# Top-k attention and an ELU layer on one core: weights decoded in two passes, and the first eight steps in written order

## The chip, the cores and the metric

The kernel runs on one core of a Trainium2 chip. The metric is the device time of one execution in microseconds (us), the median of several runs. Engines are called as in the profile: PE (TensorE, matrix products), PEld (its weight loads), DVE (VectorE), ACT (ScalarE), POOL (GpSimd) and SP (SyncE, which issues nearly all DMAs here). Each engine works through its own queue in order and waits at an instruction until what it needs from other engines is there.

## The reference

Attention over 8 batches, 8 heads, 576 tokens and 64 elements per head, in which each query keeps only the 32 largest scores of its row; then a layer with an ELU between two products.

```python
scores = scale * np.matmul(q, k.transpose(0, 1, 3, 2))        # (8, 8, 576, 576)
kth = np.partition(scores, -32, axis=-1)[..., -32:-31]
scores = np.where(scores >= kth, scores, -1e9)
attn = np.exp(scores - max); attn = attn / (sum + 1e-9)        # max and sum along the row
x = np.matmul(attn, v)           # then (B,H,S,D) -> (4608, 512)
h = x @ w_in                     # (4608, 512) @ (512, 2048)
g = np.where(h > 0.0, h, np.exp(np.minimum(h, 0.0)) - 1.0)
out = (g @ w_out).astype(np.float32)   # (4608, 2048) @ (2048, 512)
```

q, k and v are float32. `w_in` and `w_out` come as float64 (a float32 array times a float64 scalar); the kernel sees each as pairs of 32-bit words and makes float32 of them on the chip. This is the decoding that the change is about.

## The kernel before

**Steps.** A step is one tile of 128 queries for a pair of heads, so two rows of 128 x 576 scores, called row 0 and row 1 here. There are 144 steps. The first 16 take batch 0's four tiles one after the other, four head pairs each, so that the first tile's rows of x are complete after four steps and the second product's work can begin. `tight` is 8: the first eight steps have a code of their own.

**What a step goes through.** `scores` (L322) has PE multiply q by k, and ACT copy the result with the scale into an SBUF tile `sc`. The selection on DVE finds the 32nd largest score: four times the eight largest (MAX8), and between them three times the replacement of those eight by -1e30 (MATCH_REPLACE8, into `wk`). `mask` (L389) has ACT do Prelu and Exp per row, with the sum in `den`; in the first steps ACT also computes the gap between the largest and the 32nd score (L404), later POOL does (L406). `normalise` (L412) is POOL's: the reciprocal of the sum, and two multiplications of 128 x 576. `turn` (L429) transposes the row pair on PE, in nine blocks, and ACT copies them to `et`. `attend` (L454) multiplies by v on PE, and `finish` has ACT copy the result to `xT`. When a block of queries is complete, `ffn_pieces` (L521) adds its 16 pieces `hidden` (product with `w_in`, three ACT operations for each four, a gate that DVE adds up at L517, or POOL) and four `project` per 128 queries (product with `w_out`) to the list `ffn`.

**Feeding.** `feed` (L661) is called four times in a step. It takes pieces from `ffn` at a pace that spreads the work up to the time when the next block is ready (`ready`, in steps), and takes none whose weights are not decoded yet (`decoded`). It also closes gates that were opened `keep` calls before.

**Decoding.** The 32 pieces of weights (16 of each matrix, 512 KB of words, 128 x 512 results) pass through `decode_piece(i)` (L211), which loads piece i+3 and does one stage each of several pieces: `convert_first` of piece i (POOL clamps the upper words, L176), `convert_second` of piece i-1 (ACT: L182 makes a float of the lower words, L183 takes the absolute value of the upper ones into the place of the lower, L185 writes the sign into the top byte of each result), `convert_third` of piece i-3 (DVE shifts, L189), `convert_last` of piece i-4 (POOL adds, L193). Eight buffers hold raw pieces. `hook` (L199) runs the next such call: four times a step in steps 0 to 6 (after the second and third replacement of each row), not in step 7, three times a step from step 8 on. From piece 28 on, the last two stages lie one call later. There are 37 calls, so the decoding ends in step 10.

**Order.** Around the first eight steps there is no written order: the framework's scheduler places the instructions of PE, ACT, DVE and POOL, and may bring an instruction forward past others. In these steps one row is selected after the other in the program (`select_row`), both rows are masked in the same step, the transposes of step n are in the middle of step n+1, and scores are computed three steps ahead. From step 8 on (L729), the four engines run in the order that the program is written in (`manual_schedule`): both rows in turns (`select`), row 0 masked after the first pass of the next step and row 1 after the second, normalised at that step's end, and transposed a step later still. SP's order is the scheduler's throughout.

Of the kernel before, what the change touches and what calls it, by code (L numbers as in the profile page):

```python
# [10 lines left out]
FP32 = mybir.dt.float32  # L11
U32 = mybir.dt.uint32
I32 = mybir.dt.int32
FP8 = mybir.dt.float8e4
PSUM = bass.MemoryType.PSUM

TOP_K = 32
# [64 lines left out]
def kernel(  # L82
# [94 lines left out]

    def convert_second(i):
        lo, hi = parts(raw[i])
        ef = hi.bitcast(FP32)  # L180
        w = weight(i)[1]
        nc.scalar.activation(w, lo, AF.Copy, scale=2.0**-35, bias=2.0**17)  # L182
        nc.scalar.activation(lo.bitcast(FP32), ef, AF.Abs, scale=2.0**-112)  # L183
        signs = w.bitcast(FP8).rearrange("p (n w) -> p n w", w=4)[:, :, 3]
        nc.scalar.activation(signs, ef, AF.Copy, scale=2.0**-30, saturate=False)  # L185

    def convert_third(i):
        lo = parts(raw[i])[0]
# [5 lines left out]

    decode = []
    decoded = [0]
    scheduled = 4 * (2 * NHP - 1)

    def hook():  # L199

# [10 lines left out]
    def decode_piece(i):  # L211
        if i + 3 < 2 * NF:
            load_weight(i + 3)
        apart = 1 if i >= scheduled else 0
        stages = [(0, convert_first), (1, convert_second)]
        if i != scheduled:
            stages += [(3 + apart, convert_third), (4 + apart, convert_last)]
        for ago, stage in stages:
            if 0 <= i - ago < 2 * NF:
                stage(i - ago)  # L220
        decoded[0] = max(0, i - 3 - apart)

    loaded, kqT, vT = {}, {}, {}

# [85 lines left out]
    def start_qk(b, hp):  # L310
        turning.append(transpose_qk(b, hp))
# [29 lines left out]
                wide[i][:, :, 0:HS], AF.Copy, scale=scale,  # L341
            )

    def select_row(u, i, decoding):
        if i == 0:
            u.first = small.tile([P, 2, 8], FP32, tag="m1", name="m1")
            u.last = small.tile([P, 2, 8], FP32, tag="m4", name="m4")
        sc = u.sc[:, i, :]
        m = u.first[:, i, :]
        nc.vector.max(m, sc)  # L350
        wk = wkpool.tile([P, S], FP32, tag=f"wk{i}", name="wk")
        cur = sc
        for r in range(TOP_K // 8 - 1):
            nc.vector.match_replace(wk[:], m, cur, TAKEN)
            cur = wk[:]
            if r < TOP_K // 8 - 2:
                m = small.tile([P, 8], FP32, tag=f"m{i}", name="m")[:]
            else:
                m = u.last[:, i, :]
            nc.vector.max(m, cur)  # L360
            if r > 0 and decoding:
                hook()
            if r != 1:
                yield

    def select(u):

        u.first = small.tile([P, 2, 8], FP32, tag="m1", name="m1")
        u.last = small.tile([P, 2, 8], FP32, tag="m4", name="m4")
        cur = [u.sc[:, i, :] for i in range(2)]  # L370
        found = [u.first[:, i, :] for i in range(2)]
        for i in range(2):
            nc.vector.max(found[i], cur[i])  # L373
        yield
        wk = [wkpool.tile([P, S], FP32, tag=f"wk{i}", name="wk")[:] for i in range(2)]
        for r in range(TOP_K // 8 - 1):
            for i in range(2):
                nc.vector.match_replace(wk[i], found[i], cur[i], TAKEN)  # L378
            cur = wk
            for i in range(2):  # L380
                if r < TOP_K // 8 - 2:
                    found[i] = small.tile([P, 8], FP32, tag=f"m{i}", name="m")[:]
                else:
                    found[i] = u.last[:, i, :]
                nc.vector.max(found[i], cur[i])  # L385
            hook()
            yield
# [214 lines left out]
    for b in range(B):  # L602
        if b % 2 == 0:
            rest = 2 * J
            division = [(0,), (1,), (2,), (3,), (rest,), (4, 5), (6, 7)]
            if b > 0:
                division = [(0, 1), (2, 3), (rest, 4, 5), (6, 7)]
            slots = {}
            for part in division:
                blk = Block(len(blocks), len(part))  # L610
                blocks.append(blk)
                slots.update((x, (blk, s)) for s, x in enumerate(part))
        first[b] = len(steps)
        tiles = []
        for qt in range(J + 1):
            r0 = b * S + (JP if qt == J else qt if b == 0 else qt * P)
            if qt == J:
                (blk, slot), c0, n = slots[rest], (b % 2) * R, R
                rows = slice(r0, r0 + R)
            else:  # L620
                (blk, slot), c0, n = slots[(b % 2) * J + qt], 0, P
                rows = slice(r0, r0 + J * (P - 1) + 1, J) if b == 0 else slice(r0, r0 + P)
            c0 += slot * P
            t = Tile(b, qt, rows, blk, slice(c0, c0 + n))
            blk.left += NHP
            blk.tiles[slot].append(t)
            tiles.append(t)
        order = [(0, 1), (2, 3), (J,)] if b % 2 == 0 else [(J,), (0, 1), (2, 3)]
        if b == 0:
            order[:2] = [(0,), (1,), (2,), (3,)]  # L630
        for qts in order:
            for hp in range(NHP // 2 if qts == (J,) else NHP):
                group = Group([tiles[qt] for qt in qts], hp)
                steps += [Step(tiles[qt], hp, group, i) for i, qt in enumerate(qts)]
            for qt in qts:
                n = len(steps)
                tiles[qt].block.ready = n + 1.0 if n <= tight else n + 2.5
    NS = len(steps)
    total = 0.0
    for blk in sorted(blocks, key=lambda x: x.ready):  # L640
# [20 lines left out]
    def feed(n, share):  # L661

        place[0] += 1
        close_gates(2 if n < tight - 1 or n > tight + 1 else 6)
        fed["at"] = max(fed["at"], n)
        ahead = [(w - fed["sum"]) / (x - fed["at"]) for x, w in due if x > fed["at"]]
        if ahead:
            fed["over"] += max(0.0, share * min(ahead))
        fed["at"] += share
        while ffn and decoded[0] >= ffn[0][1] and 0.5 * ffn[0][0] <= fed["over"]:  # L670
            cost, _, piece = ffn.pop(0)
            fed["over"] -= cost
            fed["sum"] += cost
            piece()

    E = mybir.EngineType
    engines = {E.PE, E.Activation, E.DVE, E.Pool}
    load_qk(0, 0, nc.scalar)
    load_weight(0)
    load_qk(0, 1)  # L680
    load_weight(1)
    load_v(0, 0)
    load_weight(2)
    with tc.manual_schedule(engines=engines):
        for hp in range(2):
            start_qk(0, hp)
            turn_qk(True)
            scores(steps[hp])
    load_qk(0, 2)
    load_qk(0, 3)  # L690
    for hp in range(1, NHP):
        load_v(0, hp)
    decode += [lambda i=i: decode_piece(i) for i in range(2 * NF + 5)]
    at(0, start_qk, 0, 2)
    at(1, start_qk, 0, 3)

# [5 lines left out]
    for n in range(NS + 3):  # L702
        for fn, args in todo.pop(n, []):
            fn(*args)
        ahead, cur, prev, done = step(n + 2), step(n), step(n - 1), step(n - 2)
        if n < tight:
            turn_qk(True)
            if n < 3:
                scores(ahead)
            if n > 1:  # L710
                scores(step(n + 3))
            for i in range(2):
                passes = select_row(cur, i, n < tight - 1)
                next(passes)
                if i == 0:
                    while closing:
                        attend(closing.pop(0))
                elif prev:
                    normalise(prev)
                    turn(prev, main)  # L720
                    turn(prev, rest)
                    turn(prev, other)
                feed(n, 0.25)
                next(passes)
                mask(cur, i, True)
                feed(n, 0.25)
            continue
        if n == tight:
            ctx.enter_context(tc.manual_schedule(engines=engines))  # L729
        passes = select(cur) if cur else iter(range(4))  # L730
        if ahead and n > tight:
            scores(ahead)
        while closing:
            attend(closing.pop(0))
        next(passes)
        feed(n, 0.25)
        if prev:
            mask(prev, 0)
        turn_qk()
        next(passes)  # L740
        feed(n, 0.25)
        if done:
            turn(done, main)
            turn(done, rest)
        if prev:
            mask(prev, 1)
        next(passes)
        feed(n, 0.25)
        if done:
            turn(done, other)  # L750
        next(passes)
        if prev:
            normalise(prev)
        feed(n, 0.25)
        turn_qk(True)
    while ffn:
        ffn.pop(0)[2]()
    close_gates()
# [33 lines left out]
```

## Time and profile before

| | us |
|---|---|
| median of three runs (1642.33, 1642.60, 1644.14) | 1642.6 |
| span of the profiled execution, first to last instruction | 1640.8 |
| profiled execution's own time, as far as it is shown: its span; the median of the runs lies above it by | 1.8 |
| PE busy in the span | 1581.7 (96%) |
| DVE busy | 1453.4 (89%) |
| ACT busy | 1187.7 (72%) |
| POOL busy | 708.7 (43%) |
| chain that ended last: PE 76%, ACT 12%, DVE 7%, POOL 3% | |

The page cuts the span into 40 slices of 41 us and gives each engine's busy share in tenths, and the clock that PE was granted. Other views used below: the busy time of each engine in chosen stretches, the waits by engine, and the timeline, whose lines give start, duration, engine, line, operation, output and input, and in brackets how long the engine had idled before and for whom. The weights are decoded in the first 150 us.

The selections of steps 0 to 15 start (first maximum of each row) at 15.5, 25.1, 34.4, 45.4, 56.5, 68.3, 82.1, 97.5, 110.4, 129.7, 141.7, 152.5, 168.6, 178.2, 189.2 and 201.3 us. In steps 1 to 8 the second row starts 2 to 8 us after the first.

### The profile page before, as it was taken

The page shows a single profiled execution, that of the slowest core. Times are in us where ns is not written, and L with a number is a line of the kernel's source. Part 1 is how long each engine was busy: PE and PEld are TensorE (multiplying, and loading weights), DVE is VectorE, ACT ScalarE, POOL GpSimd, SP SyncE. Part 2 cuts the span into 40 slices and gives each one's busy share as a digit, 9 for nine tenths or more (in the row PEclk, how much of TensorE's full clock was granted, in tenths as well). Part 3 has the DMA queues.
Part 4 walks back from the last instruction along what each step waited for, and adds up shares of the span by engine and source line. Part 5 has one row for each costly group of instructions (what it writes and reads, how often), then busy time and mean ns, then how long its engine had stood idle before and what let it go on. Part 6 is the DMA issues. An engine that isn't in the chain of part 4 may idle for free.

```text
span 1640.8 us, 25344 instructions
## 1 busy us (share of the span) xinstructions
PE 1581.7 (96%) x8276; PEld 1011.8 (62%) x8276; DVE 1453.4 (89%) x2981; ACT 1187.7 (72%) x2400; POOL 708.7 (43%) x1534
## 2 busy tenths in 40 slices
PE   4788999999999999999999999999999999999999
PEld 3566777666575757555566666655557575755564
DVE  6987999999999999999999699999999599998000
ACT  6887778778695867778678686868759595958521
POOL 4775445445353534445335353535435353534300
PEclk8579999999999999999999999999999999999999
DMA  7431221012100310012100211012100201000000
GB/s 226 151 128 25 50 40 26 7 22 45 42 1 7 59 42 8 7 22 44 36 14 15 43 30 28 1 28 44 36 14 0 43 1 35 1 13 2 7 13 14
DMA packets 188037, 56.18 MB, mean 34 GB/s; under 512 B 178177, under 2 KB 179201, under 8 KB 187905
## 3 DMA queue, kind: packets, MB, share of 16 engines
q1 hardware_dynamic: 186704, 54.26, 14.1%
q8 instruction: 66, 1.08, 0.3%
q14 instruction: 67, 0.54, 0.1%
q10 hardware_dynamic: 1200, 0.30, 0.1%
HBM read 45.09 MB, written 9.44 MB: 33 GB/s over the span
## 4 chain that ended last, share of the span: by engine, by line
PE 76%; ACT 12%; DVE 7%; POOL 3%; issue 1%; DMA 1%; SPq 0%; ACTq 0%; DVEq 0%; POOLq 0%
PE ops L573 29%; PE hps L545 23%; PE avps L470 10%; PE scps L331 7%; PE eps L444 6%; DVE wk L378 3%; DVE m L385 3%; ACT sc L408 2%; ACT et L445 2%; ACT sc L407 2%; DVE m L373 1%; ACT n L564 1%; ACT n L555 1%; ACT sc L339 1%; ACT n L560 1%
## 5 line engine op out<-in xcount | busy, mean ns | idle before, releaser
L385 DVE MAX8 m<-wk 128x8 f32<-128x576 f32 x816 | 577.9, 752 | 0.3 <-POOL den L406 0.3
L545 PE MATMUL hps<-xT,w_in 128*128 128x256 f32 (+2 forms) x2432 | 545.8, 374 | 0.0
L573 PE MATMUL ops<-w_out,gT 128*128 128x512 f32 x1152 | 523.6, 599 | 0.0
L545 PEld LDWEIGHTS hps<-xT,w_in 128*128 128x128 f32 x2432 | 406.0, 192 | 100.1 <-issue 26.3
L378 DVE MATCH_REPLACE8 wk<-m,wk 128x576 f32<-128x576 f32 x544 | 401.4, 748 | 0.0
L573 PEld LDWEIGHTS ops<-w_out,gT 128*128 128x128 f32 x1152 | 209.0, 190 | 233.9 <-issue 232.8
L418 POOL TENSOR_SCALAR dene<-den 128x2 f32<-128x2 f32 x144 | 32.9, 228 | 686.5 <-ACT sc L408 686.1
L408 ACT ACTIVATE sc<-sc,den 128x576 f32<-128x576 f32 x288 | 223.6, 776 | 65.5 <-POOL den L406 44.2
L407 ACT ACTIVATE sc<-sc,m 128x576 f32<-128x576 f32 x288 | 225.3, 782 | 10.8 <-DVE m L385 10.7
L470 PE MATMUL avps<-et,vT 128*64 128x256 f32 (+2 forms) x2080 | 207.2, 330 | 17.4 <-ACT et L445 17.2
L425 POOL TENSOR_SCALAR sc<-sc,rec 128x576 f32<-128x576 f32 x288 | 213.0, 750 | 15.0 <-POOL rec L423 0.2
L331 PE MATMUL scps<-kqT 64*128 64x288 f32 (+1 forms) x1280 | 206.0, 442 | 13.6 <-ACT kqT L307 9.1
L339 ACT ACTIVATE sc<-scps 128x576 f32<-128x576 f32 x288 | 171.8, 647 | 65.1 <-PE scps L331 65.1
L445 ACT COPY et<-eps 128x512 f32<-128x512 f32 x288 | 164.6, 571 | 73.4 <-PE eps L444 73.4
L378 DVE MATCH_REPLACE8 wk<-m,sc 128x576 f32<-128x576 f32 x272 | 200.6, 748 | 0.0
L373 DVE MAX8 m<-sc 128x8 f32<-128x576 f32 x272 | 191.6, 749 | 8.8 <-ACT sc L339 8.8
L444 PEld LDWEIGHTS eps<-ident,sc 128*128 128x128 f32 x1152 | 144.9, 144 | 87.2 <-issue 52.7
L444 PE MATMUL eps<-ident,sc 128*128 128x128 f32 x1152 | 177.1, 279 | 13.7 <-POOL sc L425 13.7
L470 PEld LDWEIGHTS avps<-et,vT 128*64 128x64 f32 x2080 | 128.5, 142 | 98.8 <-ACT et L445 31.7
L515 POOL TENSOR_TENSOR gT<-n,gT 128x512 f32<-128x512 f32 (+1 forms) x119 | 164.9, 1386 | 31.2 <-ACT n L564 31.1
L331 PEld LDWEIGHTS scps<-kqT 64*128 64x128 f32 (+1 forms) x1280 | 111.3, 182 | 89.5 <-issue 43.8
L555 ACT ACTIVATE n<-hps 128x512 f32<-128x512 f32 (+1 forms) x156 | 87.3, 559 | 56.8 <-PE hps L545 56.0
(53 smaller groups left out, 1089.6 us busy)
## 6 DMA issues: line engine op xcount, KB each, us to landing
raw<-in_moe_w_in_dram SPq DMA_DIRECT2D x16, 512.0 KB, 6.1
vT<-in_v_dram SPq DMA_DIRECT2D x64, 128.0 KB, 2.5
raw<-in_moe_w_out_dram SPq DMA_DIRECT2D x16, 512.0 KB, 3.6
out_dram<-osb SPq DMA_DIRECT2D x32, 256.0 KB, 2.1
kin<-in_k_dram SPq DMA_DIRECT2D x112, 72.0 KB, 2.5
qin<-in_q_dram SPq DMA_DIRECT2D x112, 72.0 KB, 2.6
kin<-in_k_dram SPq DMA_DIRECT2D x8, 128.0 KB, 4.5
vT<-in_v_dram SPq DMA_DIRECT2D x64, 16.0 KB, 2.2
```

What stands on the lines that cost most here:

```text
L331: nc.tensor.matmul(wide[i][rows, half, 0:HS], kq[part, q0 : q0 + u.t.ql], kq[part, k0 : k0 + HS], start=True, stop=True,)
L373: nc.vector.max(found[i], cur[i])
L378: nc.vector.match_replace(wk[i], found[i], cur[i], TAKEN)
L385: nc.vector.max(found[i], cur[i])
L407: nc.scalar.activation(sc, sc, AF.Prelu, scale=-1.0, bias=low, alpha=1.0 / STEEP)
L408: nc.scalar.activation(sc, sc, AF.Exp, scale=-STEEP, bias=gap, accum_out=u.den[:, i : i + 1])
L425: nc.gpsimd.tensor_scalar(u.sc[:, i, :], u.sc[:, i, :], rec[:, i : i + 1], 1.0, ALU.mult, ALU.mult)
L444: nc.tensor.transpose(ps[:, c * P : (c + 1) * P], sc[:, c0 : c0 + P], ident[:])
L445: nc.scalar.copy(g.et[:, chunks, u.at, :], ps[:, 0 : n * P].rearrange("p (c q) -> p c q", c=n),)
L470: nc.tensor.matmul(ps[i * D : (i + 1) * D, cols], vt[:, 2 * J + i if c == J else i * J + c, :], w, start=(c == 0), stop=(c == J),)
L545: nc.tensor.matmul(blk.h[:, f % bank, :], w_in[:, i, f * P : (f + 1) * P], blk.xT[:, i, 0:n_tok], start=(i == 0), stop=(i == NC - 1),)
L573: nc.tensor.matmul(blk.o[:], blk.gT[f // NG][:, f % NG, s * P : (s + 1) * P], w_out[:, f, :], start=(f == 0), stop=(f == NF - 1),)
```

## The change

- The second stage of the decoding has two ACT operations instead of three: Copy writes the lower words' part as integers, and a Prelu of the upper words with a steep slope for negative values (`alpha` = 2^32) carries the sign along, so that the pass that wrote the sign byte is gone.
- All steps run in written order on PE, ACT, DVE and POOL, the first scores included. `select_row` is gone; the first eight steps use `select`, with rows in turns, and get a fourth hook behind the first maxima.
- Two hooks run ahead of step 0, and each of the first eight steps has four. With 36 calls the decoding ends in step 8. The last two stages always lie three and four calls behind the first.
- In the first eight steps a step's rows are masked in the next step, normalised after its third pass and transposed at its end. Scores are computed two steps ahead.
- In steps up to 8 ACT computes the gap, as before; the times at which the first two blocks count as ready move by a quarter step; gates stay open for six feeds up to step 11 instead of in steps 7 to 9 only.

```diff
     def convert_second(i):
         lo, hi = parts(raw[i])
-        ef = hi.bitcast(FP32)
-        w = weight(i)[1]
-        nc.scalar.activation(w, lo, AF.Copy, scale=2.0**-35, bias=2.0**17)
-        nc.scalar.activation(lo.bitcast(FP32), ef, AF.Abs, scale=2.0**-112)
-        signs = w.bitcast(FP8).rearrange("p (n w) -> p n w", w=4)[:, :, 3]
-        nc.scalar.activation(signs, ef, AF.Copy, scale=2.0**-30, saturate=False)
+        w = weight(i)[1].bitcast(I32)
+        nc.scalar.activation(w, lo, AF.Copy, scale=2.0**-29)
+        nc.scalar.activation(
+            lo.bitcast(FP32), hi.bitcast(FP32), AF.Prelu,
+            scale=2.0**-112, alpha=2.0**32,
+        )
...
     def decode_piece(i):
         if i + 3 < 2 * NF:
             load_weight(i + 3)
-        apart = 1 if i >= scheduled else 0
-        stages = [(0, convert_first), (1, convert_second)]
-        if i != scheduled:
-            stages += [(3 + apart, convert_third), (4 + apart, convert_last)]
-        for ago, stage in stages:
-            if 0 <= i - ago < 2 * NF:
+        stages = (convert_first, convert_second, None, convert_third, convert_last)
+        for ago, stage in enumerate(stages):
+            if stage and 0 <= i - ago < 2 * NF:
                 stage(i - ago)
-        decoded[0] = max(0, i - 3 - apart)
+        decoded[0] = max(0, i - 3)
...
-    def select_row(u, i, decoding):
...
-    def select(u):
+    def select(u, more=False):
...
         for i in range(2):
             nc.vector.max(found[i], cur[i])
+        if more:
+            hook()
         yield
...
-                tiles[qt].block.ready = n + 1.0 if n <= tight else n + 2.5
+                tiles[qt].block.ready = n + 1.25 if n <= tight else n + 2.5
...
-        close_gates(2 if n < tight - 1 or n > tight + 1 else 6)
+        close_gates(2 if n > tight + 3 else 6)
...
+    ctx.enter_context(tc.manual_schedule(engines=engines))
+    decode += [lambda i=i: decode_piece(i) for i in range(2 * NF + 4)]
     load_qk(0, 0, nc.scalar)
     load_weight(0)
     load_qk(0, 1)
     load_weight(1)
     load_v(0, 0)
     load_weight(2)
-    with tc.manual_schedule(engines=engines):
-        for hp in range(2):
-            start_qk(0, hp)
-            turn_qk(True)
-            scores(steps[hp])
+    for hp in range(2):
+        start_qk(0, hp)
+        turn_qk(True)
+        scores(steps[hp])
+        hook()
     load_qk(0, 2)
     load_qk(0, 3)
     for hp in range(1, NHP):
         load_v(0, hp)
-    decode += [lambda i=i: decode_piece(i) for i in range(2 * NF + 5)]
...
-        if n < tight:
...
-        if n == tight:
-            ctx.enter_context(tc.manual_schedule(engines=engines))
-        passes = select(cur) if cur else iter(range(4))
-        if ahead and n > tight:
+        soon = n < tight
+        passes = select(cur, soon) if cur else iter(range(4))
+        if ahead and n > 1:
             scores(ahead)
         while closing:
             attend(closing.pop(0))
         next(passes)
         feed(n, 0.25)
         if prev:
-            mask(prev, 0)
-        turn_qk()
+            mask(prev, 0, n <= tight)
+        if n > 1:
+            turn_qk()
         next(passes)
         feed(n, 0.25)
         if done:
             turn(done, main)
             turn(done, rest)
         if prev:
-            mask(prev, 1)
+            mask(prev, 1, n <= tight)
         next(passes)
         feed(n, 0.25)
         if done:
             turn(done, other)
+        if prev and soon:
+            normalise(prev)
         next(passes)
         if prev:
             normalise(prev)
+        if prev and soon:
+            turn(prev, main)
+            turn(prev, rest)
+            turn(prev, other)
         feed(n, 0.25)
         turn_qk(True)
+        if n < 2:
+            scores(ahead)
```

## Prediction

> **What bounds the kernel now.** I first read the span in slices on the page, then asked for the busy time of each engine by stage.
>
> ```profile
> PE   4788999999999999999999999999999999999999
> DVE  6987999999999999999999699999999599998000
> PEclk8579999999999999999999999999999999999999
> ```
> ```profile
> 0.00:111.70 111.70, 78.53 (x360) 56.04 (x361) 90.61 (x184) 88.58 (x182) 66.17 (x102) 0.71 0.57 172
> 111.70:178.20 66.50, 59.40 (x380) 44.31 (x379) 56.41 (x114) 54.69 (x111) 36.76 (x65) 0.87 0.19 46
> 178.20:500.00 321.80, 314.55 (x1943) 214.21 (x1943) 320.68 (x661) 248.74 (x506) 148.51 (x342) 0.99 0.14 28
> 500.00:1510.90 1010.90, 1003.51 (x5157) 624.73 (x5156) 970.97 (x1998) 748.22 (x1512) 434.12 (x984) 1.00 0.11 23
> ```
>
> The columns are PE, weight loads, DVE, ACT, POOL, granted clock, DMA share, GB/s. The bounds are events: 111.7 is where step 8 of the top-k selection begins (first maxima at 110.4 and 113.1), 178.2 where step 13 begins. From 178 to 500 DVE never rests (320.7 of 321.8), from 500 to 1511 PE hardly does (1003.5 of 1010.9). Nobody there has slack, and the edit leaves that program alone: the feeding rule, added up from the code, gives both kernels the same projection work by step 25 (130.5 of its units) and within 1.2 units by step 12. So a shift of step 13 should pass on to the end about one for one, and I forecast that shift. A program end at 1642.6 (median) stands 1.8 above the 1640.8 span; I take the 1.8 as fixed.
>
> In the first 178 us PE is half empty or at half clock, and DVE carries the pace: 13 steps in 162.7 us from its first maximum at 15.47. A step's selection alone takes 9.63 us (step 12 starts at 168.57, step 13 at 178.20). What DVE waited for there:
>
> ```profile
> DVE raw L189 <- ACT raw L183: 18.1, 4, 10.1
> DVE gT L517 <- ACT n L560: 12.0, 3, 5.7
> ```
>
> 10.1 and 3.8 us of the first row lie before the first maximum; the rest is decoding that waits for a late ACT, and gates that wait for the late projection.
>
> **Part 1: two passes for three.** A piece costs ACT L182, L183 and L185 now.
>
> ```profile
> 141.66 0.66 ACT L182 ACTIVATE w_out<-raw 128x512 f32<-128x512 uint32 x1
> 142.35 0.68 ACT L183 ACTIVATE raw<-raw 128x512 f32<-128x512 f32 x1
> 142.92 0.77 ACT L185 ACTIVATE w_out<-raw 128x512 fp8e4<-128x512 f32 x1
> ```
>
> Start to start this is 0.69 to 0.76 + 0.58 + 0.65 = 2.0. The new pair keeps the first (integers out instead of floats, same elements) and puts Prelu in L183's place. The trace has Prelu at 782 ns for 576 elements (L407, with a pointer as bias) and L183 at 677 for 512; I take 0.76 + 0.60 = 1.36, at most 1.5. Saving: 0.64 x 32 = 20.5 us of ACT, and nothing of DVE or POOL. The Trainium skill ("ScalarE: Activation LUTs", What ACT_TABLE_LOAD costs) prices all functions alike, 186 ns + 0.833 per element, thus 613 ns here, and would make the pass removed as cheap as the others, where the row has 0.77 against 0.66. No new table load is due: the trace holds one, with Prelu and Exp in turns behind it.
>
> **Part 2: the start.** Today ACT decodes pieces 0 and 1 ahead of the first scores, which go out at 14.83. In written order the first score copy follows its chain: q transposes end 8.17, copy to 8.9, scores (2.29) to 11.1, copy, so the first maximum comes at about 11.8 instead of 15.47. But the second hook's pass pair stands in ACT's queue behind the second scores (copies end near 18.5), so it ends at 19.8, and DVE's shift of piece 0, due after one round at 16.0, waits 3.8 us for it. Step 1 starts at 19.8 + 2 rounds of 2.78 + 3 shifts of 0.41 = 26.6; today its two rows start at 25.13 and 26.84. The gain is gone there.
>
> **Part 3: the queue of the loads.** SP now issues weights 3 and 4 ahead of q and k of pair 2, and weight 5 behind all of v (today the third issue ends at 11.9 and the next starts at 27.73, landing at 32.7). Two more issues of 0.6 ahead and 1 MB more to move at 300 GB/s put weight 5 at 34 to 35. DVE's shift of it (third hook of step 1, nominally at 34.2) needs POOL's clamp (0.66) and ACT's pair (1.36): about 37.2, a wait of 3, and step 2 starts near 40.7 (today 35.6, mean of the two rows).
>
> **Part 4: the loop that the written order closes.** In step n ACT's queue reads: score copies of n+2, copy to xT, pair, mask row 0 of n-1, pair, mask row 1, pair, pair, three copies of the transposes. PE's reads: scores n+2, attend n-2, transposes n-1; these wait for POOL's normalise, which waits for the second mask; and the score copies of the next step wait for PE behind those transposes. That is a ring. Rows:
>
> ```profile
> 82.46 1.47 POOL L425 TENSOR_SCALAR sc<-sc,rec 128x576 f32<-128x576 f32 x2
> 83.26 1.12 PE L444 MATMUL eps<-ident,sc 128*128 128x128 f32 x4 [4.34 <-POOL sc L425]
> 84.39 1.06 PE L444 MATMUL eps<-ident,sc 128*128 128x128 f32 x4
> 88.21 2.40 PE L470 MATMUL avps<-et,vT 128*64 128x128 f32 x18
> 140.01 0.78 ACT L407 ACTIVATE sc<-sc,m 128x576 f32<-128x576 f32 x1
> 140.88 0.78 ACT L408 ACTIVATE sc<-sc,den 128x576 f32<-128x576 f32 x1
> ```
>
> From normalise's start (80.46) to PE 2.8; nine transposes 2.2 (83.26 to 85.45); scores of both rows in turns 2.3 (as at 12.01); attend 2.65 (eighteen records in 2.40, two more at that rate); copy to xT 0.25; pair 1.36; mask 1.84 (gap 0.19, then 140.01 to 141.66); pair 1.36; mask 1.84. Sum 16.6 us a step. DVE needs 9.63 + 4 x 0.41 = 11.3, but is tied to the ring: the shift in its third pass needs the pair that ACT runs first in the same step. So DVE idles 5.3 us in each of these steps. Today's transposes also follow each other at 16 us (50.05, 67.41, 83.26, 98.60), but ACT's order there lets DVE run ahead at 12.
>
> The ring starts late. Mask row 1 of step 0 ends near 42.2; normalise, transposes, the q and k transposes of pair 3 (2.2 and 0.6), two groups of scores with their copies between (2.3 + 1.2 + 2.3 + 1.2), attend and copy (1.7 after that) and the pair end at 60.5, with 0.5 for the addition that POOL still has ahead of normalise; DVE's third shift of step 2 waits for that, and step 3 starts at 60.9 + 2.78 + 0.4 = 64.1 (today 47). Steps 3 and 4 add 16.6 each, 97.3. Steps 5 to 7 also hold 16 first-layer pieces, three ACT operations of about 0.55 for each four: 4 x 1.7 = 6.8 us, some 3 of it inside waits. Step 8 starts at 97.3 + 3 x 16.6 + 4 = 151 (today 111.7).
>
> **Part 5: steps 8 to 12.** Decoding ends in step 8 instead of 10, and gates close later (six feeds instead of two), so that DVE shouldn't wait: 5 x 9.63 + one shift 0.4 + five gates of 0.7 = 52. Today these take 66.5. POOL's queue per step (4 x 1.95 + 3.45 = 11.3) fits the ring. Rows in turns cost DVE nothing, and save PE one of two score groups of 2.29 a step (86.00 and 91.33), which does not bind. Ready times a quarter step later move 2 units: nothing.
>
> Step 13: 151 + 52 = 203, against 178.2: **+25 us**; 1642.6 + 25 = 1667.6, which I round to 1667.
>
> **A rule against a row.** The ring's PE terms are those of the half clock. The trace grants 0.50 from 40 to 95 even at full load:
>
> ```profile
> 50.00:60.00 10.00, 9.95 (x39) 6.97 (x40) 9.97 (x22) 10.00 (x21) 6.88 (x8) 0.50 0.46 129
> ```
>
> The Trainium skill ("TensorE: Matmul & The Clock Gate", What's actually happening) frees the clock after about 3.4 us of sustained work, and PE has 7.2 in a row here. By the rule the sum would be that of the second rival. The row decides.
>
> **Rivals.** (a) Faster: the ring does not close, since ACT, relieved of 0.64 a piece, keeps ahead of DVE. Then step 13 = 11.8 + 3.8 + 13 x 9.63 + 32 x 0.41 + 9 x 0.7 = 160, minus 18 us: 1624.5; with half the ring's excess left about 1637. For it: ACT's relief, and waits of 12 us on gates that go. Against: the sum; the ring would have to lose 5.3 of 16.6, and 40 us of delay by step 8 must shrink below 14.5 (what steps 8 to 12 return). That is the point from which it decides.
> (b) Slower, but mildly: PE at full clock. Scores 1.24, attend 1.45, transposes 1.2 make a ring of 13.3. Step 8 at 64.1 + 5 x 13.3 + 3 = 134, step 13 at 186: +8, 1650. It needs the early clock at 1.0, which 111 us of trace don't show.
> (c) Slower still: first-layer work in the ring at half clock (eighteen records 3.66, and its ACT operations uncovered) makes steps 5 to 7 last 16.6 + 3.7 = 20.3: step 13 at 97.3 + 61 + 52 = 210, +32, 1675.
> (d) No change: PE's later backlog swallows the shift, or (a) and the ring cancel; 1642.6. Against: DVE's full row from 178 to 500.
> The order of SP is not written by hand in either kernel; were weight 5 on time, 3 us come off, inside the range.
>
> **How the numbers follow.** Chances: forecast 0.50 (1655 to 1674), (b) 0.17, (c) 0.09, (a) 0.18, (d) 0.06. A measurement can tell 0.2%, 3.3 us: faster 0.18, same 0.06, slower 0.76. The range takes in (b), (c) and (a)'s milder half: 1636 to 1680.
>
> **What would show it.** Right: step 8's first maximum near 150, transposes in steps 2 to 6 about 16.6 apart, DVE's waits for the second pass (3.8, 3, 10.5 and five of 5.3) near 44 us, first maximum before 13, steps 8 to 12 in 52 to 55. Wrong: early steps at 11 to 12 us of DVE, a granted clock of 1.0 before 90, or a later stretch that differs.

## The result and the profile after

The changed kernel takes 1660.5 us (median of 4 runs, 1659.2 to 1661.0) where the kernel before takes 1642.5 (also four runs): 18.0 us more, a ratio of 1.0105 with a 95% interval of 1.0091 to 1.0119. The forecast was 1667. The profiled execution took 1661.0 with a span of 1659.2, so the same 1.8 us lie around the span as before.

The page's slices, of the changed kernel:

```profile
PE   3457999999999999999999999999999999999999
DVE  5779899999999999999999699999998599998100
```

In the first three slices DVE has lost one or two tenths, and PE up to three. The stages, cut at this kernel's own events (step 8 starts at 139.5, step 13 at 190.3), with the columns as before:

```profile
0.00:139.50 139.50, 64.21 (x402) 50.87 (x402) 98.31 (x193) 92.35 (x183) 78.92 (x118) 0.84 0.49 148
139.50:190.30 50.80, 44.13 (x291) 32.00 (x292) 50.80 (x105) 34.20 (x73) 21.35 (x45) 0.93 0.16 29
500.00:1510.90 1010.90, 1003.26 (x5155) 624.16 (x5155) 972.26 (x2001) 746.91 (x1510) 434.77 (x989) 1.00 0.11 23
```

The eight early steps end 29.1 us later than before (110.4 to 139.5, first maximum of step 8). The next five take 50.8 us without any idle time of DVE, which gives 17 back: step 13 stands at +12.1. From 500 us on the kernels are alike to 0.3 us of PE. No engine is full in the first row: DVE works 98 of 139.5 us, ACT 92, POOL 79. Whom DVE waits for in the first 210 us:

```profile
DVE raw L188 <- ACT raw L181: 29.2, 13, 7.7
DVE m L346 <- ACT sc L334: 11.8, 1, 11.8
```

The second row is the wait for the first scores. The first is the shift that waits for the second decoding pass, thirteen times now. A third row, 5.4 us, belongs to step 14 and comes up further below. PE's largest wait in the first 140 us is that of its transposes for POOL:

```profile
PE eps L419 <- POOL sc L400: 57.5, 6, 17.6
```

One turn of the ring, read from the timeline of step 3 (start, duration, engine, line, operation; idle time and its releaser in brackets; lines between these are left out):

```profile
65.15 1.12 PE L419 MATMUL eps<-ident,sc 128*128 128x128 f32 x4 [9.40 <-POOL sc L400]
67.26 2.29 PE L326 MATMUL scps<-kqT 64*128 64x288 f32 x8
69.49 2.02 PE L445 MATMUL avps<-et,vT 128*64 128x128 f32 x20
71.58 0.27 ACT L472 COPY xT<-avps 128x128 f32<-128x128 f32 x1 [0.80 <-PE avps L445]
71.74 0.67 ACT L180 ACTIVATE w_in<-raw 128x512 int32<-128x512 uint32 x1
72.50 0.67 ACT L181 ACTIVATE raw<-raw 128x512 f32<-128x512 f32 x1
73.20 0.67 DVE L188 TENSOR_SCALAR raw<-raw 128x512 uint32<-128x512 uint32 x1 [2.32 <-ACT raw L181]
77.10 0.78 ACT L383 ACTIVATE sc<-sc,den 128x576 f32<-128x576 f32 x1
80.95 1.11 PE L419 MATMUL eps<-ident,sc 128*128 128x128 f32 x4 [9.45 <-POOL sc L400]
```

PE runs its transposes, the scores and attend almost without a gap, then stands 9.45 us until POOL has normalised the next rows. ACT's copy waits for attend, the passes follow it, DVE's shift waits for those, and the second mask (77.10) lets POOL start. From one group of transposes to the next are 15.8 us; the later ones follow at 14.8, 15.9, 15.9 and 17.7.

### The profile page after: what moved, and what is told of

Read it like the earlier page. It is cut to its first block, busy times and chain, and to the rows that moved or that the text cites. A ratio compares the mean times of both kernels' runs of the same rounds, so it can differ in the third digit from the quotient of the medians.

```text
span 1659.2 us, 25293 instructions
## 1 busy us (share of the span) xinstructions
PE 1558.5 (94%) x8276; PEld 1001.4 (60%) x8276; DVE 1455.7 (88%) x2981; ACT 1174.3 (71%) x2368; POOL 706.8 (43%) x1534
## 4 chain that ended last, share of the span: by engine, by line
PE 79%; ACT 13%; POOL 3%; DVE 2%; issue 1%; SPq 1%; DMA 1%; ACTq 0%; DVEq 0%; POOLq 0%
PE ops L548 30%; PE hps L520 23%; PE avps L445 10%; PE scps L326 8%; PE eps L419 6%; ACT sc L383 3%; ACT sc L382 2%; ACT et L420 2%; ACT n L539 1%; ACT n L530 1%; ACT n L535 1%; ACT gT L533 1%; PE scps L419 1%; DVE wk L353 1%; POOL sc L400 1%
## 5 line engine op out<-in xcount | busy, mean ns | idle before, releaser
L360 DVE MAX8 m<-wk 128x8 f32<-128x576 f32 x864 | 609.9, 748 | 0.0
L353 DVE MATCH_REPLACE8 wk<-m,wk 128x576 f32<-128x576 f32 x576 | 423.7, 744 | 0.0
L346 DVE MAX8 m<-sc 128x8 f32<-128x576 f32 x288 | 202.3, 745 | 22.8 <-ACT sc L334 22.7
L400 POOL TENSOR_SCALAR sc<-sc,rec 128x576 f32<-128x576 f32 x288 | 212.8, 749 | 14.9
L353 DVE MATCH_REPLACE8 wk<-m,sc 128x576 f32<-128x576 f32 x288 | 211.7, 744 | 0.0
L445 PE MATMUL avps<-et,vT 128*64 128x256 f32 (+2 forms) x2080 | 196.7, 323 | 12.6 <-ACT et L420 12.5
L326 PE MATMUL scps<-kqT 64*128 64x288 f32 (+1 forms) x1280 | 192.4, 438 | 5.0 <-ACT kqT L302 3.9
L445 PEld LDWEIGHTS avps<-et,vT 128*64 128x64 f32 x2080 | 123.4, 140 | 89.3 <-issue 29.7
L326 PEld LDWEIGHTS scps<-kqT 64*128 64x128 f32 (+1 forms) x1280 | 104.2, 181 | 78.1 <-issue 44.9
L530 ACT ACTIVATE n<-hps 128x512 f32<-128x512 f32 (+1 forms) x156 | 87.0, 558 | 64.1 <-PE hps L520 63.7
```

What stands on the lines that cost most here:

```text
L326: nc.tensor.matmul(wide[i][rows, half, 0:HS], kq[part, q0 : q0 + u.t.ql], kq[part, k0 : k0 + HS], start=True, stop=True,)
L400: nc.gpsimd.tensor_scalar(u.sc[:, i, :], u.sc[:, i, :], rec[:, i : i + 1], 1.0, ALU.mult, ALU.mult)
L445: nc.tensor.matmul(ps[i * D : (i + 1) * D, cols], vt[:, 2 * J + i if c == J else i * J + c, :], w, start=(c == 0), stop=(c == J),)
```

## The experiments

Theory: the written order closes a ring over ACT, POOL and PE that paces the early steps, and the two passes are a gain by themselves. Rivals: the new pass pair is the loss; DVE's own work with its hooks is; late loads are. Each run's ratio is to the kernel before, run on the same chip. "Step 8" and "step 13" are the starts of their first maxima, 139.5 and 190.3 in the changed kernel, 110.4 and 178.2 before.

**The two passes alone.** The kernel before with the new `convert_second`:

```diff
-        nc.scalar.activation(w, lo, AF.Copy, scale=2.0**-35, bias=2.0**17)
-        nc.scalar.activation(lo.bitcast(FP32), ef, AF.Abs, scale=2.0**-112)
...
-        nc.scalar.activation(signs, ef, AF.Copy, scale=2.0**-30, saturate=False)
+        nc.scalar.activation(w, lo, AF.Copy, scale=2.0**-29)
+        nc.scalar.activation(
+            lo.bitcast(FP32), hi.bitcast(FP32), AF.Prelu,
+            scale=2.0**-112, alpha=2.0**32,
+        )
```

> The kernel before with the two-pass decoding and nothing else. Ring theory (the written order closes a ring over ACT, POOL and PE that holds DVE back; the two passes are a gain by themselves): ACT is relieved of about 0.65 us in each of 32 pieces, the scheduler's order has no ring, so the 4 us that DVE waited for the second pass in steps 0 to 10 and part of the 12 us for gates go: 1633 to 1640 us. Rival (the new pass pair is itself the loss, through Prelu's time or its clash with other engines): 1645 us or more.

Measured: 1635.7 us, ratio 0.9950 (0.9935 to 0.9965). The passes are a gain of 8 us, and this kernel beats both. Its waits of DVE in the first 220 us:

```profile
DVE raw L189 <- ACT raw L182: 20.1, 9, 10.1
DVE gT L517 <- ACT n L560: 6.4, 2, 3.9
```

DVE's waits are shorter at the gates (6.4 against 12.0), which I read as the first layer's operations no longer queueing behind a third pass; no run parts that. The shift waits no less than before (20.1 against 18.1). Step 8 even starts 6.2 us later than in the kernel before, and step 13 4.7 earlier: the gain comes in steps 8 to 12.

**Three passes in the written order**, the reverse edit on the changed kernel.

> The changed kernel with the three ACT passes of before. Ring theory: two of the four pairs of a step lie on the ring, the other two beside normalise, so 2 x 0.65 us more in each of some six rings, and about 2 us more ahead of step 1: near 1669 us, transposes 17.1 us apart instead of 15.8. Rival (the two passes are the loss): 1650 us or less. Rival (late loads set the early steps): 1660 us as it is.

Measured: 1668.6, ratio 1.0149 (1.0125 to 1.0173). The transposes of steps 2 to 7 are 17.0, 17.0, 17.1, 18.0 and 19.0 apart, and step 8 starts at 150.2. So the passes are worth 7 to 8 us in either order, and the rest of the change, the written order and the program that goes with it, costs 1.0105 / 0.9950, some 25 us, whichever passes there are.

**The scheduler's order** for the changed kernel's first eight steps:

```diff
-    ctx.enter_context(tc.manual_schedule(engines=engines))
...
+    with tc.manual_schedule(engines=engines):
+        for hp in range(2):
...
         soon = n < tight
+        if n == tight:
+            ctx.enter_context(tc.manual_schedule(engines=engines))
```

> The changed kernel with the first eight steps placed by the scheduler instead of in written order; program, hooks, two passes and gates stay. Ring theory: the scheduler brings scores, score copies and passes forward past the transposes that wait, DVE's early steps fall to 11 to 13 us, step 13 starts at 160 to 178: 1625 to 1645 us. Rival (the program itself, with four hooks a step, masks a step later and loads in another order, is the loss): 1655 us or more.

Measured: 1647.5, ratio 1.0026 (1.0016 to 1.0035); step 8 at 127.0, step 13 at 179.8. This is 2.5 us above the range and between the theories. Of the 25 us, 13 (1.0105 to 1.0026) come back when only the order is given up; the other 12 (1.0026 to 0.9950) lie in the program itself, which has its hooks, masks, turns and loads in other places than before. This run does not part these. PE's transposes still wait for POOL here, half as long as the 57.5 us of the changed kernel (first 140 us):

```profile
PE eps L419 <- POOL sc L400: 29.2, 6, 7.8
```

**The transposes a step later**, where the later steps have them, and the first blocks ready later. Six empty calls at the end of the decoding keep its buffers until step 10:

```diff
-                tiles[qt].block.ready = n + 1.25 if n <= tight else n + 2.5
+                tiles[qt].block.ready = n + 2.5
...
+    decode += [lambda: None] * 6
...
-        if prev and soon:
-            turn(prev, main)
-            turn(prev, rest)
-            turn(prev, other)
```

> The changed kernel with the transposes of the first eight steps a step later, where the later steps have them (so behind the first and second pass of the step after next); the first blocks count as ready 1.25 steps later, and the buffers of the decoding are given up in step 10. Ring theory: normalise then has a step of its own and nothing behind it waits, ACT's own 11.5 us a step bound, step 8 starts at 110 to 120 instead of 139.5, step 13 at 163 to 173: 1632 to 1645 us. Rival (hooks and DVE's tie to the second pass make the long steps): steps of 15 us stay, 1655 us or more.

Measured: 1652.8, ratio 1.0054 (1.0039 to 1.0069), 7.8 us above the range. The early part came out as the theory said: step 8 at 120.0, step 13 at 171.0, 7.2 us earlier than before the change. The total did not: the shift of a step's start against the kernel before is -8.5 us from step 15 to 48, -0.1 at step 88, +9.2 at step 120. The ready times had also moved the feeding: 127.2 of its units fed by step 25 instead of 130.5, and other pieces in other steps far into the run. The transposes and the ready times were changed at once; the next run parts them.

**The same with the ready times left at 1.25**, so that the feeding, added up from the code, is that of the changed kernel except in steps 5, 6, 12 and 13 and two of the last. Three empty calls keep the decoding's buffers until step 9.

> The changed kernel with the transposes of the first eight steps a step later, as in the run before, but with the ready times left as they are (1.25 steps), so that the feeding of projection pieces is that of the changed kernel from step 12 on; the decoding's buffers are given up in step 9. Theory: the ring is cut (step 8 at about 120, step 15 some 8 us earlier than in the kernel before), and what the run before lost again after step 48 came from its later feeding; with the feeding unchanged the shift reaches the end: 1632 to 1640 us. Rival (PE's backlog sets the end, whatever DVE gains in the early steps): 1648 us or more.

Measured: 1641.5, ratio 0.9989 (0.9980 to 0.9998). 19 us came back and the late loss is gone: the shift is -5.4 at step 13 and -5.9 at the last step. The median is 1.5 us above the range all the same; the profiled execution, 1638.5, was the fastest of its ten runs. The transposes no longer wait for POOL: PE's waits of the first 140 us have no such row (57.5 us in the changed kernel), and the timeline shows no idle time before these:

```profile
61.78 1.12 PE L419 MATMUL eps<-ident,sc 128*128 128x128 f32 x4
73.11 1.12 PE L419 MATMUL eps<-ident,sc 128*128 128x128 f32 x4
```

DVE's shift waits 10.7 us in the first 140 us, instead of 29.2:

```profile
DVE raw L188 <- ACT raw L181: 10.7, 5, 3.5
```

Steps 4 and 5 take 11.9 us there, close to DVE's own 11.3. This is the undoing that names the cause: same passes, hooks, loads and written order, but the transposes off the step in which POOL normalises.

**More POOL work in the ring**, ahead of `normalise(prev)` in the early steps:

```diff
         if prev and soon:
+            for i in range(2):
+                nc.gpsimd.tensor_scalar(
+                    prev.sc[:, i, :], prev.sc[:, i, :], 1.0, 1.0, ALU.mult, ALU.mult
+                )
             normalise(prev)
```

> The changed kernel with two more POOL multiplications by one (0.75 us each) of the same rows ahead of normalise, in the first eight steps. Ring theory: POOL has slack as a whole (11.3 of 15.8 us a step), but this time lies in the ring: 1.5 us more in each of about six rings, 1667 to 1671 us. Rival (DVE's own work with its hooks makes the long steps, or late loads do): within 2 us of 1660.5.

Measured: 1665.2, ratio 1.0135 (1.0119 to 1.0150), so 4.9 us above the changed kernel: below the 6.5 to 10.5 expected, and more than the rivals allow. Seven groups of transposes span 103.3 us instead of 99.3, 0.66 a turn. The trace shows why it is half. The first of the two multiplications needs only row 0, and is done while ACT still masks row 1; only the second stands ahead of normalise:

```profile
76.30 0.67 POOL L707 TENSOR_SCALAR sc<-sc 128x576 f32<-128x576 f32 x1 [1.22 <-ACT sc L383]
79.36 0.67 POOL L707 TENSOR_SCALAR sc<-sc 128x576 f32<-128x576 f32 x1 [2.39 <-ACT sc L383]
```

**More DVE work beside the ring**:

```diff
             nc.vector.max(found[i], cur[i])
+            if more:
+                nc.vector.max(found[i], cur[i])
```

> The changed kernel with the first two MAX8 done twice in each of the first eight steps: 1.4 us more DVE work a step, 11 us in all. Ring theory: DVE idles over 3 us in steps 2 to 7 and waits in steps 0 and 1 as well, so most is hidden: 1660 to 1665 us. Rival (DVE's own work makes the long steps): about 1671 us.

Measured: 1660.1, ratio 1.0107 (1.0092 to 1.0123): 11 us of DVE work cost nothing. The wait took it up, 19.3 us instead of 29.2:

```profile
DVE raw L188 <- ACT raw L181: 19.3, 7, 8.6
```

Together the two say that in these steps a microsecond on POOL between the second mask and the transposes costs time, and one on DVE does not.

**Scores ahead of the waiting transposes**:

```diff
-        if ahead and n > 1:
+        if ahead and n > 1 and not 2 < n <= tight:
             scores(ahead)
...
+        if 1 < n and soon:
+            scores(step(n + 3))
         if prev and soon:
             turn(prev, main)
```

> The changed kernel with the scores of step n+3 computed at the end of steps 2 to 7, ahead of the transposes that wait for normalise, instead of behind them at the start of the next step. Ring theory: the scores' 2.2 us leave the ring (PE does them while normalise runs; their copies on ACT lie there too), so the transposes are about 13.6 apart instead of 15.8, in five rings: 1647 to 1653 us. Rivals (DVE's work, loads): 1659 us or more.

Measured: 1654.9, ratio 1.0076 (1.0059 to 1.0093), 4.8 us less than the changed kernel, of 11 expected, and 1.9 above the range. The transposes are 14.7, 14.5, 14.1 and 14.9 apart. The 2.2 us of the scores did leave the ring, but attend behind the transposes grew (step 3, to be held against 2.02 and 0.80 above):

```profile
81.94 2.91 PE L445 MATMUL avps<-et,vT 128*64 128x128 f32 x20
84.89 0.27 ACT L472 COPY xT<-avps 128x128 f32<-128x128 f32 x1 [2.26 <-PE avps L445]
```

**v later**: v of head pairs 1 to 3 loaded in steps 1 to 3 of the changed kernel.

```diff
     for hp in range(1, NHP):
-        load_v(0, hp)
+        todo.setdefault(hp, []).append((load_v, (0, hp)))
```

> The changed kernel with v of head pairs 1 to 3 loaded in steps 1 to 3 instead of ahead of step 0, so that weight 5 is issued about 7 us earlier. Ring theory: the wait of 2.9 us in step 1 goes and the ring starts earlier by 3 to 6, its period stays: 1655 to 1658 us. Rival (late weights set the early steps): periods fall as well, 1650 us or less.

Measured: 1654.3, ratio 1.0070 (1.0054 to 1.0085), 0.7 below the range. Step 3 starts at 54.6 instead of 60.8, and every later step 5.8 to 6.0 earlier; the transposes from step 2 on are as far apart as in the changed kernel (15.9, 14.9, 15.9, 15.9, 17.8). So the late weight is a delay ahead of the ring, 6 us of the 18, and not its pace.

**Both: transposes and v later.**

> The previous kernel, and v of head pairs 1 to 3 loaded in steps 1 to 3 instead of ahead of step 0. Theory: the 2.9 us wait of step 1 and the late start behind it are apart from the ring, so another 3 to 6 us: 1627 to 1635 us, below both kernels and below the kernel before with two passes (1635.7). Rival (without the ring, DVE's own work or PE covers the late weight): no further gain, within 2 us of the previous kernel.

Measured: 1635.9, ratio 0.9954 (0.9937 to 0.9970); step 8 at 116.8, step 13 at 168.4. Another 5.6 us, as for v alone, though 0.9 above the range: the written order with its ring cut is 24.6 us faster than the changed kernel, and level with the scheduler's order and two passes. So with the order kept, moving the transposes (19 us) and v (6 us) gives back all of the 25.

**Gates, and v, in the kernel before with two passes.** First the later closing of gates, then v later as well:

```diff
-        close_gates(2 if n < tight - 1 or n > tight + 1 else 6)
+        close_gates(2 if n > tight + 3 else 6)
```

> The kernel before with the two-pass decoding and the later closing of gates (six feeds up to step 11). Theory: of the 6.4 us that DVE waited for gates with the two passes alone, most goes, and nothing else waits for a gate there: 1629 to 1634 us. Rival (DVE then waits at the scores or shifts instead): 1635 to 1637 us as without it.

Measured: 1635.5, ratio 0.9952 (0.9937 to 0.9966). No gain that can be told from the two passes alone, as the rival had it: step 13 comes 4.2 us earlier, and 2.0 of that is left at the last step.

> The kernel before with two passes and the later gates, and v of head pairs 1 to 3 loaded in steps 1 to 3 instead of ahead of step 0, so that POOL need not stand from 17 to 33 us for weight 3. Theory: the early decoding comes 6 us earlier, ACT is less crowded in steps 2 to 8, and DVE's steps shorten: 1627 to 1633 us. Rival (in the scheduler's order no one waits for the late weights, since DVE runs ahead of them): 1634 to 1637 us, as without it.

Measured: 1636.1, ratio 0.9962 (0.9948 to 0.9976). No gain, as the rival had it. In these runs the late weights cost time only where the written order makes others wait behind them. Four kernels at 1635.5 to 1636.1 are the fastest found.

## Why the prediction was right, and where its sizes were off

**The start, the loads, the passes** held to a microsecond: first maximum 11.82 (11.8 forecast), step 1 at 26.1 (26.6), DVE's waits for piece 0 and weight 5 3.52 and 2.92 (3.8 and 3), step 2 at 41.2 (40.7). The pass pair takes 1.33 us on ACT (71.74 to 73.07; 1.36), Prelu 0.67 for 512 elements, no more than the Abs it replaces; the 613 ns that the Trainium skill ("ScalarE: Activation LUTs", What ACT_TABLE_LOAD costs) gives for any function is somewhat under that, as it was for Abs.

**The ring** was the mechanism, and the experiments show it. Its terms, from the fence above: transposes 2.1, scores 2.2, attend 2.1, copy 0.2, pair 1.3, mask 1.75, pair 1.3, mask 1.75, normalise to PE 3.1, in all 15.8 against 16.6. What was mis-sized is Part 4's total: step 8 at 139.5, not 151. Of these 11.5 us, 3.3 lie ahead of step 3 (60.8, not 64.1): scores and attend ran there at 1.24 and 1.31, the full clock. The other 8.2 are the five steps 3 to 7, 78.7 us instead of 87. The first-layer pieces did lie in the ring, in the turns that start at 111.65 and 127.58 (1.8 us on PE in each, 1.5 on ACT in the second), but there and in the turn from 80.95 attend ran at 1.31 instead of my 2.65, and the scores at 1.24 to 2.00 instead of 2.3.

**Steps 8 to 12** took 50.8 (52). Of the signs that I named, the transposes were 14.8 to 15.9 apart and not 16.6 (17.7 in the last turn), and DVE waited 29.2 us for the second pass and not 44.

**The passing on** was the weak step. I let step 13's shift go to the end one for one. Step 13 came at +12.1 where I had +25, but the end at +18.4 by the spans. Step 14 added 4.3:

```profile
208.12 0.78 DVE L280 STREAM_TRANSPOSE kqT<-kin 128x576 f32<-128x576 f32 x1 [5.42 <-PE scps L326]
```

DVE's transpose for batch 1 waited 5.42 us for PE's scores (1.12 before). PE had nothing to do for half of the early steps, idled for less than 1 us from 150 to 200, and was behind: it began its scores in step 13 4.8 us after the step's first maximum (195.16 and 190.34), 0.7 before the change. DVE, which I followed alone, had recovered faster than PE. A further 2 us came between steps 84 and 88. The last step even starts at +21.0, and the end behind it gives 2.6 back. So the forecast of +25 met +18 with one term 12.7 too large and one 6.3 too small. That the total lay in the range was in part luck: +12.1, handed on one for one as I had it, would have been 1654.6, just below it. Between steps 15 and 84 the shift does stay at 16.4 to a tenth. In the runs with the feeding of the one kernel or the other, the shift at step 15 is the shift at the last step to 4.6 us or better; in the run with the transposes and the ready times later it moved by 16.

**The rivals.** Faster (a) needed the ring not to close; it closed. (b), the ring at full clock, came nearer than I gave it: 15.7 a step lies between 16.6 and its 13.3. The weighing of rule and row came out between them: the clock rose in every turn, but only 3.7 to 6.0 us after the transposes began. Where it rose after 3.7 us the turn took 14.8 (from 80.95), where after 5.8 and 6.0 it took 15.8 and 15.9 (from 65.15 and 95.74); the turn from 111.65 had its rise after 3.7 us too, but first-layer products in it, and took 15.9. My sign of being wrong, a clock of 1.0 before 90, did appear, from 50.50 on, but in stretches.

**What was not seen ahead:** that half of the cost stays when the order is given up and the program kept. The run with the scheduler's order shows it (1647.5 against 1635.7).

## What to carry to other kernels

When instructions are put in a written order, add up not each engine's work but the ring: follow one result through the queues until it comes back to the engine where it began, and count what each queue has in front. Here a chain of mask, normalise and transposes set the pace when one step held them all, and no longer did so once the transposes had a step of their own. To tell a ring from a full engine, add idle work to two engines: only what lies in the ring shows in the time. And when one engine's delay is carried forward, carry the other engines' backlog too.

## What the runs showed of the hardware that was not expected

In the kernel before, PE was granted half the clock for 58 us on end, though it was busy for 46 of them (start and end, length, PE busy, granted clock, DMA share, GB/s):

```profile
38.45:96.47 58.02, 46.14 (x172) 0.50 0.49 158
```

The Trainium skill's rule ("TensorE: Matmul & The Clock Gate", What's actually happening), about 3.4 us of sustained work for the full clock, does not foretell this; why, no run here shows. In the changed kernel, whose PE works in bursts of 5 to 9 us there, the clock goes up and down once in every turn:

```profile
70.98:74.39 3.41, 0.53 (x10) 1.00 0.83 262
74.39:84.63 10.24, 3.67 (x15) 0.50 0.20 64
84.63:91.46 6.83, 1.67 (x24) 1.00 0.79 254
```

It rises 3.7 to 6.0 us after the transposes begin (65.15 and 80.95 for the rises at 70.98 and 84.63), which is nearer to the rule, and so late that PE is idle for most of the two stretches at full clock shown here. The first clock record of the changed kernel is that at 50.50 us, and of the kernel before that at 21.38; the 1.00 that the views show ahead of it is no measurement. The scores at 26.09 us took 2.29, as at half clock, and those at 50.76 took 1.24.

DVE's shift of 128 x 512 takes 0.41 us alone and 1.48 when it starts just behind POOL's addition (66.61 and 66.52 us in the changed kernel), five times between 66 and 131 us. Six other shifts began later in an addition and took 0.58 to 1.19; all eleven end 0.29 us after that addition. The timeline of the first of the five pairs:

```profile
66.52 1.29 POOL L192 TENSOR_TENSOR w_in<-w_in,raw 128x512 int32<-128x512 int32 x1
66.61 1.48 DVE L188 TENSOR_SCALAR raw<-raw 128x512 uint32<-128x512 uint32 x1
```
